# One planned order for every instruction of an attention and feed-forward kernel

## The chip, the cores and the metric

The kernel runs on one core of one Trainium2 chip. The metric is device microseconds (us) of that core, lower is better. The engines are PE (matrix products), DVE (vector), ACT (activation), POOL, and SP, which here only issues DMAs. Each engine works through its own queue strictly in order; semaphores tie the queues together.

## What is computed

```python
# batch 4, heads 12, sequence 448, head size 64; model 768, hidden 2048
scores = scale * q @ k^T                         # [4, 12, 448, 448]
scores = einsum('bhij,hg->bgij', scores, w_pre)  # mixes the heads
attn = softmax(scores, axis=-1)
attn = einsum('bhij,hg->bgij', attn, w_post)     # mixes the heads again
x = (attn @ v) as [1792, 768]
h = x @ w_in                                     # the feed-forward part
out = (h * sigmoid(1.702 * h)) @ w_out
```

The weights w_in and w_out arrive as 64-bit floats, the rest as 32-bit floats.

## The kernel before

**Attention in steps.** Mixing the heads is a matrix product over (query row, head) pairs, so a step takes 10 query rows of 12 heads, 120 partitions. A batch has 45 steps, the kernel 180. The scores of a batch are made in 4 chunks of 120 query rows (the last has 88): for each of 6 pairs of heads `scores` makes two products `qk` in PSUM (tag `gen`, 3 banks), `keep_scores` copies them to a tile `sc`, and `send_scores` writes that to a DRAM buffer `sd`. For a step, `gather` reads its 120 x 448 tile `r` back from `sd`, 4 steps ahead (`AHEAD`). Then: `mix` (PE, into one of 2 banks `mx`), `peak` (DVE, row maximum), `expo` (ACT, exponential and its sum), `shifted` (POOL) and `inverse` (DVE) for the reciprocal, `weigh_mix` (POOL) for the scaled second mixing matrix, `post_whole` (PE, `pp`), and `keep_whole` (ACT), which copies the result to the tile `p` of its chunk. Batches 0 and 1 do this in 32 bits. Batches 2 and 3 carry numbers as pairs of 16-bit floats, an upper and a lower part, each product being three 16-bit ones: `weigh`, `upper`, `lower`, `post`, `keep_upper`, `keep_lower`, and q, k, v are loaded, measured (`squares`) and split (`upper_part`, `lower_part`).

**Product with v.** When a chunk's steps are through, `context` multiplies `p` with v, one pair of heads (`pr`) per call, three calls sharing one PSUM bank `av`; `x_upper`, `x_lower` and `x_size` then take the bank to the 16-bit pair `x`. When all four chunks are there, `scale_x` sets a factor, and the batch's feed-forward part may begin.

**Feed-forward in quanta.** The hidden width is cut into 8 slices; a unit is one slice for one batch (32 units). A unit is 12 quanta on PE of six 128 x 448 products each: 2 x 3 for `hidden` (`h`) and 6 for `project` (`po`). Between them `gate` (ACT, DVE, ACT, DVE) makes `g`, and `collect` adds `po` to `acc`, on DVE alone or through ACT and POOL (`pt`). Each of the 16 weight slices is first converted once: `convert` loads 64-bit numbers (`w64`, three DMAs), makes 32-bit ones with five DVE instructions a part, splits them into a 16-bit pair and stores that to DRAM (`wd`); `fetch_w` reads the pair back for every unit (`wt`).

**What sets the order.** The program is written out in the order in which the instructions are to stand (`manual_schedule`). A loop over the steps lists each step's parts in a fixed order, with fixed lags (`LAG`). Side work (loads, conversions, splits) is a list of `jobs` with a first step, dependences in whole steps, and budgets of time (`tokens`) that each step refills. Feed-forward quanta are owed at `RATE` 2.15 per step. `slot` moves every chain (`gate`, `collect`, scores, context) one stage on. In the head, before step 0, the loads of q and k of batch 0 alternate with those of the first weight slice, and the second slice follows.

Of the kernel before, what the change touches and what calls it, by code (L numbers as in the profile page):

```python
# [39 lines left out]
def attention_then_feed_forward(ctx, tc, q, k, v, w_pre, w_post, w_in, w_out, out):  # L40
# [13 lines left out]
    AHEAD, LAG = 4, 3  # L54
    OVERLAP = True
# [58 lines left out]

    def sum_jobs(first, m, parts, after):

        t = {}

        def over():
            t["t"] = add_over(parts())  # L120

        j = job(first, None, 0, over, after=after, urgent=True)
        return job(first, "D", 0.2, lambda: add_along(m(), t["t"]), after=[j], urgent=True)
# [100 lines left out]
    open_banks = []  # L224

    def bank(name, tag="gen", bufs=3):

        if tag == "gen":
            while len(open_banks) >= bufs and not open_banks[-bufs]["done"]:
                slot()  # L230
            open_banks.append({"done": False})
        return ps.tile([128, 512], F32, name=name, tag=tag, bufs=bufs)

    def scores(b, c, pr, tag=("gen", 3)):
# [3 lines left out]
        done = open_banks[-2:] if tag[0] == "gen" else []  # L238
        w = NPAIR // THIRDS
        if b < WHOLE:  # L240
            qf, kf = st["q", b, pr // w], st["k", b, pr // w]
            for x in range(2):
                rs = slice(x * D, (x + 1) * D)
                nc.tensor.matmul(  # L244
                    two[x][:n, :S], qf[rs, pr % w, i0:i0 + n], kf[rs, pr % w, :],
                    start=True, stop=True,
                )
            return two, done
# [9 lines left out]
        return two, done  # L258

    def keep_scores(b, c, pr, two, engs, home=("sc", 3)):  # L260
        i0, n = chunk(b, c)
        t = flow.tile([CI, 2, S], F32, name=f"sc_{b}_{c}_{pr}", tag=home[0], bufs=home[1])
        for x in range(2):
            (nc.scalar.copy if engs[x] == "A" else nc.vector.tensor_copy)(t[:n, x, :], two[x][:n, :S])  # L264
        return t
# [84 lines left out]
    def upper(i):  # L350
        K = rows_of(steps[i][1])[1] * H
        a1 = flow.tile([KG, S], F16, name=f"a1_{i}", tag="a1", bufs=3)
        nc.scalar.activation(a1[:K], row.pop(("e", i))[:K], AF.Copy, scale=row.pop(("rs", i))[:K, 0:1])
        row["a1", i] = a1
# [116 lines left out]
    parts = []  # L471

    stores = []
    EARLY = -20

    def convert(kind, s, first):
# [80 lines left out]
        sizes = []  # L557
        for a in range(NP):
            n = len(parts) + a
            users = []  # L560
            begin = first + a if first == EARLY else first
            before = [(job(begin, None, 0, lambda a=a: fetch(a), stage=("w64", users)), 2)]
            before += [(parts[n - WF], 0)] if n >= WF else []
            for eng, cost, f in (
                ("D", 0.37, magnitude), ("D", 0.37, least), ("D", 0.37, shift), ("D", 0.8, rest), ("D", 0.8, sign),
            ):
                last = job(first, eng, cost, lambda f=f, a=a: f(a), after=before)
                users.append(last)
                before = [(last, 0)]
            sizes.append(job(first, "A", 0.7, lambda a=a: size(a), after=[(last, 1)]))  # L570
        j = sum_jobs(first, total, lambda: t["m"], [(x, 1) for x in sizes])
        j = job(first, "D", 0.9, scale_w, after=[(j, 0)])
        low = []
        for a in range(NP):
            up = job(first, "A", 0.72, lambda a=a: w_upper(a, "A"), after=[(j, 1)] + [(x, 0) for x in stores[-1:]])
            low.append(job(first, "D", 0.7, lambda a=a: w_lower(a), after=[(up, 1)]))
        parts.extend(low)
        stores.append(job(first, None, 0, store, after=[(x, 1) for x in low]))
        return stores[-1]
# [10 lines left out]
    def hidden(u, fc, part):  # L590

        s, b = units[u]
        if part == 0:
            st["h", u, fc] = bank(f"h_{u}_{fc}")[:, :S], open_banks[-1]
        h, _ = st["h", u, fc]
# [9 lines left out]
    def gate(u, fc):  # L605

        s, b = units[u]
        h, held = st.pop(("h", u, fc))
        if fc == 0:
            gt[u] = flow.tile([128, 2, SF, S], F16, name=f"g_{u}", tag="g", bufs=2)  # L610
            st["ct", u] = stat.tile([128, 2], F32, name=f"ct_{u}", tag="ct")
            nc.vector.tensor_scalar(
                st["ct", u][:, 0:1], ex[:, b:b + 1], ew[:, s, 0:1], 0.851 * 2.0 ** -13,
                op0=ALU.mult, op1=ALU.mult,
            )
        g = gt[u]
        th = flow.tile([128, S], F32, name=f"th_{u}_{fc}", tag="th", bufs=2)
        nc.scalar.activation(th, h, AF.Tanh, scale=st["ct", u][:, 0:1])  # L618
        spend("A", 0.55)
        yield  # L620
        nc.vector.scalar_tensor_tensor(th, th, 1.0, h, op0=ALU.add, op1=ALU.mult)  # L621
        held["done"] = True
        spend("D", 0.65)
        yield
        nc.scalar.activation(g[:, 0, fc], th, AF.Copy, scale=gs[:, b, 1:2])  # L625
        spend("A", 0.55)
        yield
        nc.vector.scalar_tensor_tensor(  # L628
            g[:, 1, fc], th, gs[:, b, 1:2], g[:, 0, fc], op0=ALU.mult, op1=ALU.subtract
        )  # L630
        spend("D", 0.65)

    def project(u, e):
        g, w = gt[u], wt[1, u].rearrange("p t (f e) -> p t f e", e=DM)
        po = bank(f"po_{u}_{e}")[:, :S]
        held = open_banks[-1]
# [6 lines left out]
        return po, held  # L643

    def collect(u, e, po, held):
        s, b = units[u]
        c = st["ct", u][:, 1:2]
        if e == 0:
            nc.vector.tensor_tensor(c, eo[:, b:b + 1], ew[:, s, 2:3], op=ALU.mult)
# [3 lines left out]
        held["done"] = True  # L653
        if s == 0:
            if tokens["A"] > tokens["D"]:
                nc.scalar.activation(a, po, AF.Copy, scale=c)
                spend("A", 0.55)
            else:
                nc.vector.tensor_scalar(a, po, c, 1.0, op0=ALU.mult, op1=ALU.mult)
                spend("D", 0.62)  # L660
        elif tokens["A"] > tokens["D"] + 0.3 and tokens["G"] > -1.0 and s < NS - 1:
            pt = flow.tile([128, S], F32, name=f"pt_{u}_{e}", tag="pt", bufs=2)
            nc.scalar.activation(pt, po, AF.Copy, scale=c)  # L663
            spend("A", 0.55)
            yield
            nc.gpsimd.tensor_tensor(a, a, pt, op=ALU.add)  # L666
            spend("G", 1.3)
        else:
            nc.vector.scalar_tensor_tensor(a, po, c, a, op0=ALU.mult, op1=ALU.add)  # L669
            spend("D", 0.65)  # L670
        if s == NS - 1:
            yield
            nc.sync.dma_start(out=out[e * 128:(e + 1) * 128, b * S:(b + 1) * S], in_=a)


    tokens = {"A": 0.0, "D": 0.0, "G": 0.0}

    def spend(eng, cost):
        tokens[eng] -= cost

    def refill(t):
        for e in tokens:
            tokens[e] = min(tokens[e] + t, 4.5)

    going = []

    def start(gen):

        going.append(gen)

    def slot():
        for g in list(going):
            if next(g, g) is g:
                going.remove(g)

    jobs = []

    stage_users = {"op": [], "w64": []}

    def stage_free(tag):  # L700

        u = stage_users[tag]
        return len(u) < THIRDS or all("at" in j for j in u[-THIRDS])

    def job(first, eng, cost, f, after=(), stage=None, urgent=False):
        j = {"urgent": urgent, "first": first, "eng": eng, "cost": cost, "f": f, "stage": stage,
             "after": [a if isinstance(a, tuple) else (a, 1) for a in after]}
        jobs.append(j)
        return j

    def run_jobs(i):
        more = True
        while more:
            more = False
            for j in list(jobs):
                if j["first"] > i or any(a.get("at", 10 ** 6) + lag > i for a, lag in j["after"]):
                    continue
                if j["stage"] is not None:
                    tag, users = j["stage"]
                    if not stage_free(tag):  # L720
                        continue
                    stage_users[tag].append(users)
                eng = j["eng"]
                if isinstance(eng, dict):
                    eng = max(eng, key=lambda e: tokens[e] - eng[e])
                    cost = j["eng"][eng]
                else:
                    cost = j["cost"]
                if eng and tokens[eng] < cost * 0.5 and not j["urgent"]:
                    continue  # L730
                if eng:
                    spend(eng, cost)
                j["f"](eng) if isinstance(j["eng"], dict) else j["f"]()
                j["at"] = i
                jobs.remove(j)
                more = True


    SENT = 2

    def staged(first, after, name, b, i, use):
# [348 lines left out]
```

## Time and profile before

| | |
|---|---|
| time, median of 3 runs | 991.54 us (990.67 to 992.24) |
| profiled execution | 991.19 us, of which the profiled span is 989.3 us |
| PE busy | 921.2 us of the span (93%) |
| DVE, ACT, POOL busy | 588.6, 581.7, 313.8 us |
| DMA | 196.74 MB, mean 199 GB/s |

The span is what the trace covers; the execution's own time is 1.9 us more. PE is the busiest engine by far. Its idle time, and what it waits for, are read by stage in the rows below, because DMA is dense early and thin late.

### The profile page before, as it was taken

The numbers are of one execution on the slowest core, as the hardware profiler recorded it, in microseconds if no ns is written. First come the engines' busy times: TensorE is split into PE (matmuls) and PEld (weight loads), VectorE is DVE, ScalarE is ACT, GpSimd is POOL, SyncE is SP. The second block draws the span as 40 slices with busy tenths as digits, with TensorE's granted clock in tenths as the row PEclk, the third lists the DMA queues.
The fourth block names the chain that finished last, engine by engine and source line by source line (L and its number), as shares of the span: only waits on it lengthen the run. The fifth ranks groups of instructions, "written<-read, shape, count | busy, mean of one in ns | idle before, by whom it ended". The sixth has DMA issues, their size and how long they took to land.

```text
span 989.3 us, 18926 instructions
## 1 busy us (share of the span) xinstructions
PE 921.2 (93%) x6972; PEld 544.9 (55%) x6972; DVE 588.6 (59%) x1333; ACT 581.7 (59%) x1342; POOL 313.8 (32%) x500
## 2 busy tenths in 40 slices
PE   6688899988999999997998999998999999999998
PEld 4345565654555556564564656564555666555554
DVE  5677776667658976456556575556555555442333
ACT  2577668775677667666567666556465555223331
POOL 0122222221113423445443543335435353001221
PEclk8799999999999999999999999999999999999999
DMA  8999878976778785557666575456645332153322
GB/s 302 284 324 320 292 265 266 316 249 189 242 251 272 252 262 181 182 170 214 198 199 222 164 223 156 143 161 199 212 133 167 103 118 65 65 183 129 104 88 88
DMA packets 66175, 196.74 MB, mean 199 GB/s; under 512 B 7620, under 2 KB 32324, under 8 KB 66084
## 3 DMA queue, kind: packets, MB, share of 16 engines
q1 hardware_dynamic: 65680, 195.46, 61.0%
q8 instruction: 55, 0.90, 0.4%
q10 hardware_dynamic: 404, 0.09, 0.1%
q14 instruction: 36, 0.29, 0.1%
HBM read 138.89 MB, written 56.62 MB: 198 GB/s over the span
## 4 chain that ended last, share of the span: by engine, by line
PE 67%; DVE 16%; ACT 8%; DMA 5%; issue 3%; POOL 0%; ACTq 0%; SPq 0%; DVEq 0%
PE h L600 19%; PE po L639 19%; PE mx L290 9%; PE pp L335 4%; PE av L424 3%; PE av L413 3%; PE qk L244 2%; PE qk L254 2%; DVE nm L297 2%; DVE w_f L510 2%; ACT e L304 2%; PE pp L372 2%; PE pp L374 2%; PE pp L373 2%; DVE w_f L516 2%
## 5 line engine op out<-in xcount | busy, mean ns | idle before, releaser
L639 PE MATMUL po<-g,wt 128*128 128x448 f16 x1152 | 243.4, 355 | 13.6 <-DVE th L621 8.6
L600 PE MATMUL h<-x,wt 128*128 128x448 f16 x1152 | 241.0, 354 | 4.9 <-ACT sc L264 3.7
L290 PE MATMUL mx<-r,wa 120*120 120x448 f32 x360 | 178.3, 578 | 26.0 <-ACT e L304 16.5
L304 ACT ACTIVATE e<-mx,nm 120x448 f32<-120x448 f32 x180 | 115.6, 642 | 139.8 <-DVE rs L320 130.5
L639 PEld LDWEIGHTS <-wt 128*128 128x128 f16 x1152 | 109.8, 99 | 126.9 <-issue 42.0
L600 PEld LDWEIGHTS <-wt 128*128 128x128 f16 x1152 | 109.3, 98 | 112.6 <-issue 24.2
L669 DVE SCALAR_TENSOR_TENSOR acc<-po,ct,acc 128x448 f32<-128x448 f32 x131 | 89.1, 681 | 71.4 <-PE po L639 69.9
L359 POOL TENSOR_TENSOR a<-w,a 120x448 f16<-120x448 f32 (+1 forms) x90 | 95.9, 1065 | 102.8 <-issue 46.7
L297 DVE TENSOR_REDUCE nm<-mx 120x1 f32<-120x448 f32 x180 | 110.6, 615 | 16.4 <-PE mx L290 16.3
L618 ACT ACTIVATE th<-h,ct 128x448 f32<-128x448 f32 x64 | 40.4, 632 | 133.8 <-PE h L600 117.9
L621 DVE SCALAR_TENSOR_TENSOR th<-th,h 128x448 f32<-128x448 f32 x64 | 39.6, 619 | 128.2 <-ACT th L618 128.2
L335 PEld LDWEIGHTS pp<-wr,e 120*112 120x112 f32 x720 | 89.0, 180 | 36.5 <-issue 30.4
L264 ACT COPY sc<-qk 120x448 f32<-120x448 f32 (+1 forms) x186 | 89.6, 532 | 31.9 <-PE qk L244 22.4
L325 POOL TENSOR_SCALAR wr<-wp,rs 120x120 f32<-120x120 f32 (+1 forms) x90 | 54.8, 609 | 166.7 <-DVE rs L320 119.8
L345 POOL TENSOR_SCALAR w<-e,rs 120x448 f32<-120x448 f32 (+1 forms) x90 | 66.0, 733 | 124.5 <-DVE rs L320 70.5
L290 PEld LDWEIGHTS mx<-r,wa 120*120 120x120 f32 x360 | 60.0, 187 | 67.2 <-ACT e L304 30.6
L315 POOL TENSOR_SCALAR rs<-sm 120x1 f32<-120x1 f32 x180 | 46.7, 260 | 142.0 <-ACT e L304 132.3
L335 PE MATMUL pp<-wr,e 120*112 120x120 f32 x720 | 90.3, 269 | 0.0
L666 POOL TENSOR_TENSOR acc<-acc,pt 128x448 f32<-128x448 f32 x37 | 43.6, 1179 | 129.6 <-ACT pt L663 128.7
L372 PE MATMUL pp<-wp,a 120*112 120x120 f16 x360 | 62.4, 217 | 3.8 <-DVE p L399 1.9
L320 DVE RECIPROCAL rs<-rs 120x1 f32<-120x1 f32 x180 | 28.1, 156 | 61.8 <-POOL rs L315 61.6
L628 DVE SCALAR_TENSOR_TENSOR g<-th,gs,g 128x448 f16<-128x448 f32 x64 | 50.3, 785 | 20.8 <-ACT g L625 19.8
(126 smaller groups left out, 1337.5 us busy)
## 6 DMA issues: line engine op xcount, KB each, us to landing
wt<-wd SPq DMA_DIRECT2D x64, 768.0 KB
r<-sd SPq DMA_DIRECT2D x176, 210.0 KB
sd<-sc SPq DMA_DIRECT2D x72, 420.0 KB
w<-in_moe_w_in_dram SPq DMA_DIRECT2D x24, 512.0 KB
w<-in_moe_w_out_dram SPq DMA_DIRECT2D x24, 512.0 KB
wd<-w_p SPq DMA_DIRECT2D x16, 768.0 KB
sd<-sc SPq DMA_DIRECT2D x24, 308.0 KB
out_dram<-acc SPq DMA_DIRECT2D x24, 224.0 KB
```

Of the source, the lines that this page charges most:

```text
L264: (nc.scalar.copy if engs[x] == "A" else nc.vector.tensor_copy)(t[:n, x, :], two[x][:n, :S])
L290: nc.tensor.matmul(mx[:K, :S], st["wa", b][:K, :K], row.pop(("r", i))[:K, :], start=True, stop=True)
L297: nc.vector.tensor_reduce(nm[:K], row["mx", i][:K, :S], axis=AX.X, op=ALU.max, negate=True)
L304: nc.scalar.activation(e[:K], row.pop(("mx", i))[:K, :S], AF.Exp, bias=row.pop(("nm", i))[:K, 0:1], scale=1.0, accum_out=sm[:K, 0:1],)
L325: nc.gpsimd.tensor_scalar(t[:K], wp[:K], row.pop(("rs", i))[:K, 0:1], 1.0, op0=ALU.mult, op1=ALU.mult)
L335: nc.tensor.matmul(pp[:CP, jc * K:(jc + 1) * K], e[:K, jc * CP:(jc + 1) * CP], wr[:K, :, :n], start=True, stop=True,)
L345: nc.gpsimd.tensor_scalar(w[:K], e[:K], row["rs", i][:K, 0:1], 1.0, op0=ALU.mult, op1=ALU.mult)
L359: nc.gpsimd.tensor_tensor(a2[:K], row.pop(("w", i))[:K], row["a1", i][:K], op=ALU.subtract)
L372: nc.tensor.matmul(o, a1[:K, js], wp1[:K, :, :n], start=True, stop=False)
L600: nc.tensor.matmul(h, w[:, i, c, fc * 128:(fc + 1) * 128], x[:, j, c, :], start=(n == 0), stop=(n == len(terms) - 1),)
L639: nc.tensor.matmul(po, w[:, j, fc, e * 128:(e + 1) * 128], g[:, i, fc, :], start=(n == 0), stop=(n == len(terms) - 1),)
L669: nc.vector.scalar_tensor_tensor(a, po, c, a, op0=ALU.mult, op1=ALU.add)
```

## The change

All scheduling code (`job`, `run_jobs`, `slot`, `tokens`, `do_quantum`) goes. Every piece of work becomes a task with its engine or a choice of engines, the time that it holds the engine (`occ`), the time until its result may be used (`lat`), the buffers that it takes, and a due step. `run_all` replays these on model clocks and writes out one task after another: on each engine, among the tasks that could start within 0.1 us of the earliest, the one with the earliest due step; of all engines the one that starts first. DMAs are modelled too, at 0.31 MB a us and with 8 in flight. The work itself is that of before, with these differences:

- Head: q and k of batch 0 are loaded first and alone; the conversions of weights begin in step 1 (slice n at 7n instead of 7n - 12, the first two before step 0). The scores of chunk 0 are sent in two parts, rows 0 to 47 of all six pairs, then the first four gathers, then the other rows. The three small loads of w_pre and w_post move from ACT's queue to SP's.
- The three calls of `context` for a bank are one task.
- Copies of scores may go to ACT or DVE, results to DVE or to ACT and POOL, splits to POOL or ACT, as the plan finds. Against before, ACT makes 150 score copies instead of 186 and DVE 42 instead of 6; 64 additions of `pt` run on POOL instead of 37, and 104 on DVE instead of 131.
- The feed-forward part is due from step 57 at 2.13 quanta a step.

```diff
-    OVERLAP = True
+    AHEAD = 4
...
-    def send_scores(b, c, pr, t):
-        n = chunk(b, c)[1]
-        nc.sync.dma_start(out=sd[b, c][:, 2 * pr:2 * pr + 2, :], in_=t[:n])
+    def send_scores(b, c, pr, t, lo=0, hi=CI):
+        hi = min(hi, chunk(b, c)[1])
+        nc.sync.dma_start(out=sd[b, c][lo:hi, 2 * pr:2 * pr + 2, :], in_=t[lo:hi])
...
+    def run_all():
+        last = ""
+        while waiting:
+            picks = []
+            for e in list(free) + ["-"]:
+                best = []
+                for j in waiting:
+                    if e not in j["eng"]:
                         continue
+                    room = room_for(j, e)
+                    if room is None:
+                        continue
+                    s = max(room, j["from"], free.get(e, 0.0))
+                    if j["size"] and len(lanes) >= 8:
+                        s = max(s, lanes[-8])
+                    best.append((s + (j["bias"] if e != j["eng"][0] else 0.0), s, j))
+                if best:
+                    t = min(x[0] for x in best) + LOOK
+                    picks.append(min((x for x in best if x[0] <= t), key=lambda x: (x[2]["due"], x[0]))[1:] + (e,))
+            s, j, e = min(picks, key=lambda x: (x[0], x[1]["due"]))
...
     for i in range(THIRDS):
         for name in "kq":
             load_whole(name, 0, i)
-        run_jobs(EARLY + i)
...
     for pr in range(NPAIR):
-        two, done = scores(0, 0, pr, tags[pr % 3])
-        send_scores(0, 0, pr, keep_scores(0, 0, pr, two, "AD", homes[pr]))
+        two = scores(0, 0, pr, tags[pr % 3])
+        kept.append(scores_home(0, 0, pr, homes[pr]))
+        for x in range(2):
+            keep_scores(0, 0, x, kept[pr], two, "AD"[x])
+        send_scores(0, 0, pr, kept[pr], 0, FRONT)
...
     for i in range(AHEAD):
         gather(i)
-    for i in range(THIRDS):
-        load_whole("v", 0, i)
+    for pr in range(NPAIR):
+        send_scores(0, 0, pr, kept[pr], FRONT)
...
+            def product(half=half, t=t):
+                for pr in range(3 * half, 3 * half + 3):
+                    t["av"] = context(b, c, pr)
```

**SP's queue in the head.** These are the last sends of chunk 0's scores (`sd`), the loads of the second weight slice (`w`), and the first gathers (`r`); the same stretch of before and of the change:

```order
L269 DMA sd_0_90<-sc_0_4_216 120x896
L269 DMA sd_0_90<-sc_0_5_224 120x896
L489 DMA w_0_64_0_234<-in_moe_w_out_dram 128x1024
L489 DMA w_0_64_1_237<-in_moe_w_out_dram 128x1024
L489 DMA w_0_64_2_239<-in_moe_w_out_dram 128x1024
L280 DMA r_241<-sd_0_90 120x448
L280 DMA r_243<-sd_0_90 120x448
```

```order
L250 DMA sd_0_90<-sc_0_4_190 48x896
L250 DMA sd_0_90<-sc_0_5_198 48x896
L261 DMA r_215<-sd_0_90 120x448
L261 DMA r_217<-sd_0_90 120x448
L261 DMA r_219<-sd_0_90 120x448
L261 DMA r_221<-sd_0_90 120x448
L250 DMA sd_0_90<-sc_0_0_158 72x896
```

Behind the shorter sends come the gathers at once; the other 72 rows of each send follow them, and the weights stand further back.

**PE's queue in batch 0, chunk 0 before and chunk 1 after.** `av` is the product with v, `mx` a step's mixing, `pp` its second mixing, `qk` scores:

```order
L413 MATMUL av_0_0_884<-p_0_417,vf_0_251 64x120 x8
L290 MATMUL mx_982<-r_848,wa_255 120x448
L335 MATMUL pp_984<-wr_949,e_907 112x120 x4
L413 MATMUL av_0_3_1009<-p_0_417,vf_0_251 64x120 x8
L290 MATMUL mx_1025<-r_894,wa_255 120x448
L335 MATMUL pp_1027<-wr_996,e_946 112x120 x4
L244 MATMUL qk_3_1_0_1053<-kf_0_122,qf_0_124 88x448
L244 MATMUL qk_3_1_1_1054<-kf_0_122,qf_0_124 88x448
L413 MATMUL av_0_3_1009<-p_0_417,vf_0_253 64x120 x8
```

```order
L271 MATMUL mx_1106<-r_1019,wa_203 120x448
L394 MATMUL av_1_0_1113<-p_1_799,vf_0_364 64x120 x16
L394 MATMUL av_1_0_1113<-p_1_799,vf_0_409 64x120 x8
L271 MATMUL mx_1160<-r_1027,wa_203 120x448
L316 MATMUL pp_1173<-wr_1156,e_1141 112x120 x4
```

Three runs of 8 products with other work between them have become one run of 24.

**DVE's queue where v of batch 2 is split.** `vp` is the lower part of v, `th` and `g` belong to `gate`, `nm` and `rs` to a step, `p` is `keep_lower`:

```order
L297 TENSOR_REDUCE nm_5231<-mx_5181 120x1
L320 RECIPROCAL rs_5196<-rs_5196 120x1
L212 SCALAR_TENSOR_TENSOR vp_2_5198<-vb_2_5110,s_v_4359,vp_2_5198 112x1024
L212 SCALAR_TENSOR_TENSOR vp_2_5200<-vb_2_5112,s_v_4359,vp_2_5200 112x1024
L212 SCALAR_TENSOR_TENSOR vp_2_5202<-vb_2_5114,s_v_4359,vp_2_5202 112x1024
L612 TENSOR_SCALAR ct_5289<-ex,ew 128x1
L621 SCALAR_TENSOR_TENSOR th_0_5291<-th_0_5291,h_0_5248 128x448
```

```order
L201 SCALAR_TENSOR_TENSOR vp_2_5194<-vb_2_5091,s_v_4204,vp_2_5194 112x1024
L576 SCALAR_TENSOR_TENSOR th_0_5230<-th_0_5230,h_0_5143 128x448
L301 RECIPROCAL rs_5245<-rs_5245 120x1
L201 SCALAR_TENSOR_TENSOR vp_2_5249<-vb_2_5096,s_v_4204,vp_2_5249 112x1024
L586 SCALAR_TENSOR_TENSOR g_5271<-th_0_5230,gs,g_5271 128x448
L278 TENSOR_REDUCE nm_5301<-mx_5251 120x1
```

The three long splits no longer stand together; `th`, for which the projections wait, has moved in between.

## Rows read from the trace of the kernel before

**Rows 1.** Page, part 1: busy us (share of the span) xinstructions.
```profile
span 989.3 us, 18926 instructions
...
PE 921.2 (93%) x6972; PEld 544.9 (55%) x6972; DVE 588.6 (59%) x1333; ACT 581.7 (59%) x1342; POOL 313.8 (32%) x500
```

**Rows 2.** Page, part 4: the chain that ended last, by engine.
```profile
PE 67%; DVE 16%; ACT 8%; DMA 5%; issue 3%; POOL 0%; ACTq 0%; SPq 0%; DVEq 0%
```

**Rows 3.** Five stretches: start:end, length, then what the first row names.
```profile
core 0: us, PE busy (x) PEld busy (x) DVE busy (x) ACT busy (x) POOL busy (x), PEclk, DMA share, GB/s
0.00:31.00 31.00, 16.40 (x79) 11.35 (x79) 18.10 (x47) 7.37 (x16) 0.70 (x7) 0.81 0.90 305
31.00:199.60 168.60, 148.57 (x980) 93.14 (x980) 121.63 (x309) 123.85 (x313) 38.97 (x103) 0.97 0.87 294
199.60:357.00 157.40, 146.33 (x944) 87.75 (x943) 114.16 (x273) 106.23 (x257) 38.82 (x68) 0.97 0.73 239
357.00:824.90 467.90, 450.27 (x3908) 267.62 (x3907) 270.40 (x578) 292.91 (x667) 205.89 (x294) 0.99 0.57 176
824.90:989.30 164.40, 159.66 (x1066) 85.07 (x1064) 64.31 (x129) 51.38 (x90) 29.40 (x29) 1.00 0.32 109
```

**Rows 4.** Waits of PE, 31 to 199.6, then to the end: total, times, longest.
```profile
PE mx L290 <- ACT e L304: 15.3, 17, 1.7
...
PE po L639 <- DVE th L621: 8.6, 5, 3.6
```

**Rows 5.** SP's issues and PE's first mixing in the head: start, us, what.
```profile
19.99 2.99 SPq L489 DMA_DIRECT2D w<-in_moe_w_out_dram  x3
24.48 2.20 SPq L280 DMA_DIRECT2D r<-sd  x4
...
30.90 3.31 PE L290 MATMUL mx<-r,wa 120*120 120x448 f32 x4 [7.97 <-DMA r<-sd]
```

**Rows 6.** Gathers issued up to 183 us; mixings (two records each) up to 206 us.
```profile
L280 SPq DMA_DIRECT2D r<-sd x52: 316/360/1263, 24.5 to 182.3; - x52
...
L290 PE MATMUL mx<-r,wa x108: 539/627/1071, 30.9 to 200.1; 120*120 120x448 f32 x106, 96*96 96x448 f32 x2
```

**Rows 7.** PE in order of time, three pieces: start us, us, what.
```profile
131.63 0.98 PE L335 MATMUL pp<-wr,e 120*112 120x120 f32 x8
132.54 1.04 PE L413 MATMUL av<-p,vf 112*64 112x120 f32 x16
133.51 1.01 PE L290 MATMUL mx<-r,wa 120*120 120x448 f32 x2
134.36 0.98 PE L335 MATMUL pp<-wr,e 120*112 120x120 f32 x8
...
222.07 0.98 PE L335 MATMUL pp<-wr,e 120*112 120x120 f32 x8
222.89 3.57 PE L600 MATMUL h<-x,wt 128*128 128x448 f16 x18
...
440.40 0.92 PE L290 MATMUL mx<-r,wa 120*120 120x448 f32 x2
441.16 1.30 PE L639 MATMUL po<-g,wt 128*128 128x448 f16 x6
```

**Rows 8.** DVE, then PE, about 460 us in order of time.
```profile
458.05 5.71 DVE L212 SCALAR_TENSOR_TENSOR vp<-vb,s_v,vp 112x1024 f16<-112x1024 f32 x3
...
465.33 3.65 PE L639 MATMUL po<-g,wt 128*128 128x448 f16 x12 [3.58 <-DVE th L621]
```

**Rows 9.** One line of DVE and one of POOL: ns min/median/max.
```profile
L628 DVE SCALAR_TENSOR_TENSOR g<-th,gs,g x64: 662/683/1556, 235.4 to 978.3; 128x448 f16<-128x448 f32 x64
...
L666 POOL TENSOR_TENSOR acc<-acc,pt x37: 1129/1132/1590, 285.2 to 979.5; 128x448 f32<-128x448 f32 x37
```

More of the change, by code (lines that the diff above doesn't have):

```diff
@@ L247, in scores @@
                 )
-            return two, done
+            return two
         qp, kp = st["qp", b, pr // w], st["kp", b, pr // w]
@@ L555, in store @@
             nc.sync.dma_start(out=wd[kind, s], in_=t["p"])
[L557 to L579, printed above, removed]
+        return {"fetch": fetch, "magnitude": magnitude, "least": least, "shift": shift, "rest": rest, "sign": sign,
+                "size": size, "total": total, "parts": lambda: t["m"], "scale_w": scale_w, "w_upper": w_upper,
+                "w_lower": w_lower, "store": store}
     units = [(s, b) for b in range(B) for s in range(NS)]
@@ L678, in spend @@
[L678 to L703, printed above, removed]
@@ new lines, in take, with settle @@
+    def take(j, e):
+        for x in j["takes"]:
+            if len(x) == 2 or x[2] == e:
+                have = held[x[0]]
+                if len(have) >= COUNT[x[0]]:
+                    done = [(over_when(h), n) for n, h in enumerate(have) if over_when(h) is not None]
+                    have.pop(min(done)[1])
+                have.append(x[1])
+    def settle(j, at, e, gap):
+        j["at"] = at
+        for x in j["next"]:
+            x["left"] -= 1
+            if not x["left"]:
+                waiting.append(x)
+        for x in j["then"]:
+            x["from"] = max(x["from"], at + (0.0 if e == "-" else SAME if x["eng"] == (e,) else gap))
+            x["left"] -= 1
+            if not x["left"]:
+                waiting.append(x)
@@ new lines, in score_tasks, with product, place @@
+    def score_tasks(b, c, pr, x):
+        third = pr // (NPAIR // THIRDS)
+        banks, sc, t = [[], []], [], {}
+        def product():
+            t["two"] = scores(b, c, pr)
+        def place():
+            t["t"] = scores_home(b, c, pr)
+        j = add("PE", 0.84 if b < WHOLE else 0.61, product,
+                gated_by(x) + [inputs.get((n, b, third)) for n in "kq"], x + 0.2, takes=[("gen", h) for h in banks], kind="qk")
+        for n in "kq":
+            in_home[n, b, third].append(j)
+        h = add("-", 0.0, place, [j], x + 0.3, 0.0, takes=[("sc", sc)])
+        both = []
+        for n in range(2):
+            k = add("A/D", {"A": 0.42, "D": 0.53}, lambda e, n=n: keep_scores(b, c, n, t["t"], t["two"], e), [h], x + 0.3,
+                    {"A": 0.53, "D": 0.62}, bias=0.3)
+            banks[n].append(k)
+            both.append(k)
+        s = add("SP", 0.4, lambda: send_scores(b, c, pr, t["t"]), both, x + 2, size=0.43)
+        sc += both + [s]
+        sends.setdefault((b, c), []).append(s)
```

702 lines of the change are left out of this document (382 added, 320 removed).

## The prediction, made before the changed kernel ran

> **What bounds the kernel now.** I read the busy shares first, then the chain, then the stretches, then the waits. PE is busy 93% of the span [rows 1] and holds 67% of the chain that ended last, against 16% for DVE and 5% for DMA [rows 2]: the end is set by how early PE gets through its work. But the mean hides stages. In the stretches [rows 3] the reader is to compare PE's busy time with the length, and then DMA's share: up to 199.6 us, when the 54th of 180 mixings starts [rows 6], DMA engines are 0.87 to 0.90 busy at about 300 GB/s and PE idles 34.6 us (14.6 of them in the first 31); from 357 us on PE idles 22.4 us in 632, and DMA is at 0.57 and below. So the first fifth is limited by DMA and PE together, the rest by PE. The waits [rows 4] say what PE lacks: early the exponential of a step (15.3 us in 17 waits; two banks for mixings, so a mixing waits for the exponential two steps back), later mostly `th`, the gate of the feed-forward part.
>
> **The change part by part.** The work is the same, so no instruction's price goes away; what can change is what stands ahead of what. Four terms.
>
> *1. The head and the first 53 mixings.* Before, the first gather is issued at 24.48 us, behind three loads of the second weight slice that take SP 2.99 us to issue, and the first mixing, which waited 7.97 us for the gathers, starts at 30.9 [rows 5]. By the queue's order six weight loads (6 x 0.524 = 3.15 MB by their shape) leave the front; at the 305 GB/s of that stretch [rows 3] they are 10.3 us. The first sends shrink to 48 of 120 rows, but the rest follows right behind the gathers and delays the fifth gather, and PE must still make the last scores first. I take 9 us for the head at the least. The other bound is DMA's: adding up the shapes of all DMAs ahead of the 53rd gather gives 55.6 MB before and 50.9 MB after, since conversions begin later. Before, 52 gathers were out by 182.3 us [rows 6], the 53rd by about 184 (estimate), 0.302 MB a us; at that rate 4.7 MB less are 15 us. Between 9 and 15 I take 12: PE would have to do its 148.6 us of work of the second stretch [rows 3] in about 163 us instead of 168.6, 91% instead of 88%, which needs only a third of the 15.3 us of waits for exponentials to go. If those waits stay, it is 9.
>
> *2. Products with v in threes, and fewer changes of kind.* The reader is to take start-to-start times [rows 7]. `pp` ahead of a product with v takes 0.91 us (131.63 to 132.54), ahead of `h` 0.82 (222.07 to 222.89); a mixing behind a product with v takes 0.85 (133.51 to 134.36), behind `po` 0.76 (440.40 to 441.16). So entering or leaving a run of `av` or `qk` costs about 0.09 us each way. PE's queue has 340 such borders before and 234 after; from the 54th mixing on, 246, and 159 after the change from the same place (its first `h`). 87 x 0.09 = 7.8 us; the other 19 are part of term 1. The cost is a later start of the bank's first copy, by two products of 0.97 us [rows 7]; one bank serves `av`, but a chunk lasts 12 steps, so this is hidden.
>
> *3. Work done ahead.* At that place 24 products with v (pairs of heads) are done instead of 20, and 50 second mixings instead of 49: 4 x 0.88 + 0.82 = 4.3 us less are left, 0.88 being the single run's 0.97 less one border. The feed-forward part starts there, behind 53 mixings, and not behind 60. From mixing 60 to 180 both orders place 253 quanta, so the pace per step stays; 5 more quanta are already done before, inside these steps' gaps.
>
> *4. Stalls behind 199.6 us.* PE idles 11.1 + 17.6 + 4.7 us in the last three stretches [rows 3]; the last 4.7, in which nearly only feed-forward work is left, I count as staying. Of the 28.7, the most telling piece is at 460 us [rows 8]: three splits of v hold DVE 5.71 us without a break, `th` waits behind them, and PE stands 3.58 us. The planned queue puts `th` and steps between those splits. PE pays twice: the 12 `po` behind this gap took 3.65 us, where 18 `h` take 3.50 elsewhere [rows 7]. The granted clock is 0.97 and 0.99 in the two stretches [rows 3], 4.7 us lost in each (0.03 x 157.4 and 0.01 x 467.9). A plan on fixed durations cannot remove all of this: I take half of the idle time (14.3) and half of the clock's (4.7), 19 us, with bounds of 0 and 38.
>
> What the plan moves between engines I cost at nothing: 36 score copies go from ACT to DVE and 27 additions from DVE to ACT and POOL, on engines that are 59%, 59% and 32% busy [rows 1]. If PE waits for them it costs up to their own length each, about 0.7 us. One row speaks against more work on POOL: the lower part of g on DVE has a median of 683 ns and a maximum of 1556, and POOL's addition takes 1132 [rows 9], so now and then DVE seems held for most of a POOL instruction. The Trainium skill, SBUF — State Buffer, section SBUF: two separate sides, says that a DVE operation with two SBUF inputs and a POOL operation that reads SBUF lock each other out for a whole instruction; by it 27 more additions could hold DVE 27 x 1.13 = 31 us, were each to meet one. By the row most do not (the median stands near the minimum). I keep it out of the sum, as DVE idles 400 us.
>
> Sum, on the profiled span: 989.3 - 12 - 7.8 - 4.3 - 19 = 946.2; the execution's time is 1.9 us more than its span (991.19 against 989.3), and the median of the runs, 991.54, agrees with it. **948 us**, 4.4% faster.
>
> **The rivals.**
>
> *The plan holds almost to the letter.* The estimate for the start becomes 20 us (the 15 by DMA, and some more from the exponentials' waits), and all of term 4's 38 goes: 989.3 - 20 - 7.8 - 4.3 - 38 + 1.9 = 921. For it: the plan's durations for PE are those of the rows (its code has 0.84 us for `pp`, the rows 0.82). Against: it has one number per instruction where DVE's spread is twofold [rows 9], and one rate for DMA.
>
> *Only the switches are saved.* Real latencies differ from planned ones, and in strict queues each error becomes a stall of the old size: terms 1 and 4 are zero. 989.3 - 7.8 - 4.3 + 1.9 = 979.
>
> *DMA falls behind the plan, and the kernel is slower.* The plan counts on 0.31 MB a us. Ahead of the 90th gather stand 96.2 MB after the change (102 before). Rows 3 give 9.5 + 49.6 + 37.6 = 96.7 MB moved by 357 us, 0.271 MB a us; the 90th gather of before went out at about 370 us (estimate: 102 MB, less than 8 DMAs in flight). If the new mixture of reads and writes moved only the 0.239 of the third stretch, the gather would come at 402 us, 32 later. About 14 us of terms 2 and 4 lie behind that place, so 989.3 + 32 - 14 + 1.9 = 1009. It decides from an average rate below 96.2 / 384 = 0.25 MB a us. For it: mixings, and all behind them on PE, wait for gathers in order. Against: the 0.239 was measured while PE was 93% busy and asked for no more, and 0.294 and 0.305 are seen where more was asked [rows 3].
>
> *No change.* Stalls moved, not removed, and the head's gain lost in the wait for later conversions: by the queues' order the last slice's weights are now fetched two steps ahead of their first use, where it was three. It gives 990.
>
> **How the numbers follow.** Forecast 0.50 (its own range 935 to 965), plan to the letter 0.20, only switches 0.17, DMA behind 0.10, no change 0.03. The predicted time is the forecast's. The range leaves out the slower rival (0.10) and the low edge of the best case (0.10): 918 to 985. About 0.2% is what a measurement of this kernel can tell from no change; faster by more than that 0.87, within it 0.03, slower 0.10.
>
> **What would show it.** Term 1: the first mixing at about 22 us, the first `h` at about 188, and DMA still near 0.9 busy until then. Term 2: PE's start-to-start times as above, `av` in runs of three at about 0.9 us a pair. Term 4: PE's idle time behind the first `h` at about 19 us instead of 33, the waits for `th` at a few us, a granted clock nearer 1.00. The prediction is wrong if gathers end PE's waits through the first 350 us, if PE's idle time stays or grows behind the first `h`, or if PE's work on the same products takes longer than now.

## The result, and the profile after

The changed kernel takes 930.92 us (median of 4 runs, 929.78 to 934.01), the kernel before 991.89 (990.67 to 994.66): a ratio of 0.9387 [0.9356, 0.9418]. The forecast of 948 us was 17 us too high, and its own range of 935 to 965 missed the time by 4; the whole range of 918 to 985 held it. The profiled execution took 930.12 us, 928.4 of them span, 60.9 less than before.

The page, part 1 and part 4, against [rows 1, 2]:

```profile
span 928.4 us, 18998 instructions
...
PE 897.2 (97%) x6972; PEld 535.5 (58%) x6972; DVE 589.4 (63%) x1342; ACT 593.3 (64%) x1328; POOL 337.8 (36%) x532
...
PE 75%; DVE 9%; DMA 6%; ACT 5%; issue 2%; POOL 2%; SPq 1%; ACTq 0%; POOLq 0%; DVEq 0%
```

PE makes the same 6972 products, but is busy 24.0 us less and idle 31.2 us instead of 68.1. DVE's share of the chain fell from 16% to 9%. Five stretches, columns as in [rows 3]; they end at the first mixing, at the first `h`, and then where like parts of the program end:

```profile
0.00:19.00 19.00, 13.89 (x76) 10.36 (x77) 6.27 (x19) 4.68 (x8) 0.71 (x7) 1.00 0.73 229
19.00:180.50 161.50, 147.95 (x1027) 93.13 (x1028) 117.26 (x300) 116.80 (x292) 35.69 (x101) 0.96 0.91 302
180.50:330.00 149.50, 146.78 (x959) 90.09 (x959) 129.19 (x318) 113.60 (x277) 43.38 (x78) 1.00 0.87 285
330.00:768.00 438.00, 433.94 (x3928) 259.61 (x3925) 284.16 (x601) 298.94 (x653) 213.57 (x305) 1.00 0.61 191
768.00:928.40 160.40, 154.60 (x996) 82.29 (x990) 52.49 (x108) 59.32 (x100) 44.46 (x42) 1.00 0.32 109
```

The first `h`, which here follows 53 mixings, starts at 180.5 us; before, the 54th mixing started at 199.6. That is 19.1 us; the rest of the gain lies behind this place. The same view of everything behind it, first of the kernel before, then of the changed one:

```profile
199.60:989.30 789.70, 756.25 (x5916) 440.44 (x5914) 448.87 (x979) 450.52 (x1013) 274.12 (x390) 0.99 0.55 174
```

```profile
180.50:928.40 747.90, 735.33 (x5871) 431.99 (x5869) 465.84 (x1025) 471.87 (x1029) 301.41 (x424) 1.00 0.60 192
```

41.8 us less, of which 21.0 are PE's busy time and 20.8 its idle time (33.4 to 12.6). In the second stretch DMA moves 302 GB/s, before 294: the rate is hardly higher. The granted clock is 1.00 behind the first `h`, but 0.96 in the second stretch, before 0.97.

The waits of PE, whole run (total, times, longest), against [rows 4]:

```profile
PE pp L316 <- POOL wr L306: 6.0, 10, 1.1
PE mx L271 <- DMA r<-sd: 3.1, 2, 2.7
PE h L557 <- DMA wt<-wd: 2.9, 1, 2.9
...
PE po L595 <- DVE th L576: 2.4, 3, 1.4
...
PE mx L271 <- ACT e L285: 1.9, 3, 0.8
```

The wait for exponentials fell from 15.3 us in the early stretch alone to 1.9, that for `th` from 8.6 to 2.4. None of those left is over 6 us in all. The head in order of time, against [rows 5]:

```profile
16.14 1.68 SPq L261 DMA_DIRECT2D r<-sd  x4
...
19.00 0.98 PE L271 MATMUL mx<-r,wa 120*120 120x448 f32 x2 [2.66 <-DMA r<-sd]
```

The gathers leave 8.3 us earlier, and the first mixing starts 11.9 us earlier. PE around a product with v, against [rows 7]:

```profile
109.50 0.98 PE L316 MATMUL pp<-wr,e 120*112 120x120 f32 x8
110.42 2.68 PE L394 MATMUL av<-p,vf 112*64 112x120 f32 x48
113.32 1.07 PE L316 MATMUL pp<-wr,e 120*112 120x120 f32 x8 [0.23 <-POOL wr L306]
114.23 0.92 PE L271 MATMUL mx<-r,wa 120*120 120x448 f32 x2
```

Three pairs of heads now stand in one run of 2.68 us, 0.89 a pair; before, a pair took 0.97 with its border.

### The profile page after: what moved, and what is told of

It is laid out like the page before. It is cut to its first block, busy times and chain, and to the rows that moved or that the text cites. A ratio compares the mean times of both kernels' runs of the same rounds, so it can differ in the third digit from the quotient of the medians.

```text
span 928.4 us, 18998 instructions
## 1 busy us (share of the span) xinstructions
PE 897.2 (97%) x6972; PEld 535.5 (58%) x6972; DVE 589.4 (63%) x1342; ACT 593.3 (64%) x1328; POOL 337.8 (36%) x532
## 4 chain that ended last, share of the span: by engine, by line
PE 75%; DVE 9%; DMA 6%; ACT 5%; issue 2%; POOL 2%; SPq 1%; ACTq 0%; POOLq 0%; DVEq 0%
PE po L595 20%; PE h L557 20%; PE mx L271 12%; PE pp L316 5%; PE av L394 3%; PE av L405 3%; PE qk L225 3%; PE qk L235 3%; DMA r<-sd 2%; PE pp L353 2%; PE pp L355 2%; PE pp L354 2%; DVE nm L278 2%; ACT e L285 1%; ACT waste L96 1%
## 5 line engine op out<-in xcount | busy, mean ns | idle before, releaser
L557 PE MATMUL h<-x,wt 128*128 128x448 f16 x1152 | 246.8, 352 | 3.2 <-DMA wt<-wd 2.9
L271 PE MATMUL mx<-r,wa 120*120 120x448 f32 x360 | 172.3, 563 | 5.2 <-DMA r<-sd 3.1
L623 POOL TENSOR_TENSOR acc<-acc,pt 128x448 f32<-128x448 f32 x64 | 72.8, 1138 | 117.3 <-ACT pt L617 116.9
L340 POOL TENSOR_TENSOR a<-w,a 120x448 f16<-120x448 f32 (+1 forms) x90 | 95.8, 1064 | 26.3 <-POOL w L326 17.6
L246 ACT COPY sc<-qk 120x448 f32<-120x448 f32 (+1 forms) x150 | 74.5, 532 | 15.7 <-PE qk L225 11.3
L619 DVE SCALAR_TENSOR_TENSOR acc<-po,ct,acc 128x448 f32<-128x448 f32 x104 | 70.3, 679 | 22.0 <-PE po L595 21.1
L326 POOL TENSOR_SCALAR w<-e,rs 120x448 f32<-120x448 f32 (+1 forms) x90 | 60.5, 672 | 40.8 <-DVE rs L301 35.0
L617 ACT ACTIVATE pt<-po,ct 128x448 f32<-128x448 f32 x64 | 40.6, 634 | 51.1 <-PE po L595 51.0
L334 ACT ACTIVATE a<-e,rs 120x448 f16<-120x448 f32 (+1 forms) x90 | 60.3, 670 | 18.4 <-DVE rs L301 17.2
L380 DVE TENSOR_TENSOR p<-pp,p 112x480 f16<-112x480 f32 (+1 forms) x90 | 58.4, 649 | 19.2 <-ACT p L376 18.9
L306 POOL TENSOR_SCALAR wr<-wp,rs 120x120 f32<-120x120 f32 (+1 forms) x90 | 47.4, 527 | 54.0 <-DVE rs L301 33.7
```

Source lines behind the costliest of these rows:

```text
L246: (nc.scalar.copy if eng == "A" else nc.vector.tensor_copy)(t[:n, x, :], two[x][:n, :S])
L271: nc.tensor.matmul(mx[:K, :S], st["wa", b][:K, :K], row.pop(("r", i))[:K, :], start=True, stop=True)
L326: nc.gpsimd.tensor_scalar(w[:K], e[:K], row["rs", i][:K, 0:1], 1.0, op0=ALU.mult, op1=ALU.mult)
L340: nc.gpsimd.tensor_tensor(a2[:K], row.pop(("w", i))[:K], row["a1", i][:K], op=ALU.subtract)
L557: nc.tensor.matmul(h, w[:, i, c, fc * 128:(fc + 1) * 128], x[:, j, c, :], start=(n == 0), stop=(n == len(terms) - 1),)
L623: nc.gpsimd.tensor_tensor(a, a, st.pop(("pt", u, e)), op=ALU.add)
```

## The experiments

Twelve kernels. A difference between two of them is that of their ratios to the kernel before, times 992 us; 0.003 in a ratio (3 us) is about half an interval's width.

**1. Products with v one at a time, the rest as changed** (337 borders on PE instead of 234; a border is a place in PE's queue where the kind of product changes to or from `av` or `qk`).

```diff
-                for pr in range(3 * half, 3 * half + 3):
-                    t["av"] = context(b, c, pr)
+            for pr in range(3 * half, 3 * half + 3):
+                def product(pr=pr, t=t):
+                    t["av"] = context(b, c, pr)
+                j = add("PE", 0.87 if whole else 0.6, product, ...)
```

> The changed kernel with its products with v planned one pair of heads at a time again (three tasks per bank, due 0.8 steps apart), all else replanned. PE's queue then has 337 borders of qk or av runs instead of 234. Theory of the borders (0.09 us each on a PE that is hardly idle): 103 x 0.09 = 9 us slower than 930.9, so 940, with PE's idle time about as it is (31 us in all). Rival 1, the products in threes gain nothing because PE's gaps swallow the borders: 931 +- 2. Rival 2, the longer hold of PE by a run of three was itself delaying the steps: 925 or less.

942.34 us, ratio 0.9476 [0.9443, 0.9509]: 8.8 us more than the changed kernel. PE in order of time (start, us):

```profile
102.42 1.04 PE L394 MATMUL av<-p,vf 112*64 112x120 f32 x16
103.39 1.01 PE L271 MATMUL mx<-r,wa 120*120 120x448 f32 x2
104.33 1.04 PE L394 MATMUL av<-p,vf 112*64 112x120 f32 x16
105.30 1.01 PE L271 MATMUL mx<-r,wa 120*120 120x448 f32 x2
106.15 0.98 PE L316 MATMUL pp<-wr,e 120*112 120x120 f32 x8
```

A mixing between two products with v takes 0.94 from start to start (103.39 to 104.33), one that only follows such a product 0.85 (105.30 to 106.15), as in [rows 7]. 103 more borders of 0.09 us make 9.3, and the median is 8.8 us longer: the price of a border agrees, and under the plan the end moves by about as much. The trace does not part it from the clock: PE is 14.4 us longer busy (911.6 against 897.2) at a granted clock of 0.985 instead of 0.992, and idles 2.5 us less.

**2. Products with v in threes, the rest as before.**

```diff
-at_context.setdefault(last + LAG + 2 + pr, []).append((b, c, pr))
+at_context.setdefault(last + LAG + 4 + 3 * (pr // 3), []).append((b, c, pr))
```

> The kernel before, order by hand, with three products with v of a bank put together in one step (the third step of before's three for the first bank, so that no due time moves earlier). 236 borders instead of 340. Theory of the borders: 104 x 0.09 = 9 us of PE time less, 981 to 985, if the run of three does not delay the steps. Rival, that the hand order's gaps swallow it, or that the bank's later copies give it back: 989 to 994.

988.81 us, 0.9973 [0.9957, 0.999]: 2.7 us gained by 104 fewer borders, where 9.4 were to come. That is at the edge of the rival's 989. PE's busy time fell by 5.7 us only (921.2 to 915.5), at a granted clock of 0.973 instead of 0.981, and these waits grew:

```profile
PE mx L290 <- ACT e L304: 20.4, 24, 3.1
PE po L639 <- DVE th L621: 9.8, 7, 3.6
```

PE's idle time as a whole grew by 1.5 us. That a run of 2.7 us pushes back the mixing behind it in the fixed order, and so makes these waits, is my reading. So term 2 exists by itself, but kept a third of its size without the plan; of what is missing, the trace has 3.7 us as busy time, at the lower clock, and 1.5 as idle time.

**3. The plan on wrong durations**, each multiplied by a random factor from 0.6 to 1.4.

```diff
+        wrong = rng.uniform(0.6, 1.4)
+        occ, lat = {e: o * wrong for e, o in occ.items()}, {e: o * wrong for e, o in lat.items()}
         j = {"eng": tuple(occ), "occ": occ, "lat": lat, "f": f,
```

> The changed kernel planned with wrong durations: each task's engine time and latency times a random factor between 0.6 and 1.4 (DMAs stay as they were). The work, the due steps and the buffers are the same, and 235 borders instead of 234. Theory that the plan's accuracy is what removed PE's idle time: the idle time goes back to the old size or above (68 us of the span before, 31 after the change), 965 to 985. Rival, that the graph with its due steps and small borders is enough and engine queues forgive errors of this size: within 1% of 930.9, below 940.

937.57 us, 0.9427 [0.9398, 0.9456]: 4.0 us more, and the intervals still overlap. The wait for `wr` grew to 10.9 us, the largest. My theory that accurate durations removed the idle time fell; an order from the graph of tasks and the due steps does most of it: in this trace PE idles 41.1 us, before 68.1 and with the right durations 31.2. It is one draw of the factors.

**4. The three lower splits of a tensor a step apart, the rest as before.**

```diff
-                         after=[(up, 1)], urgent=True)
+                         after=[(up, 1)] + ([(lo, 1)] if lo else []), urgent=True)
```

> The kernel before, order by hand, with the three lower parts of a split (k, q, v of batches 2 and 3) put at least one step apart on DVE instead of back to back. Theory of term 4's example: PE's gaps of 3.58 us at 465 and 3.47 us at 690 us, where th waits behind 5.7 us of splits, go, and with them the slow clock behind each (about 1.2 us each): 7 to 10 us less, 982 to 985. Rival, that the stall moves to whatever comes late next: 988 to 993.

983.34 us, 0.9909 [0.9889, 0.9928]: 9.0 us gained by this alone, as expected. At the place of [rows 8] in the kernel before, `th` needs `ct`, a small factor that DVE makes behind the three splits and ACT waits for (DVE, ACT, DVE):

```profile
463.69 0.20 DVE L612 TENSOR_SCALAR ct<-ex,ew 128x1 f32<-128x1 f32 x1
463.99 0.63 ACT L618 ACTIVATE th<-h,ct 128x448 f32<-128x448 f32 x1 [2.96 <-DVE ct L612]
464.65 0.62 DVE L621 SCALAR_TENSOR_TENSOR th<-th,h 128x448 f32<-128x448 f32 x1 [0.76 <-ACT th L618]
```

The wait for `th`, and DVE at this place, with the splits apart:

```profile
PE po L639 <- DVE th L621: 3.7, 5, 1.5
```

```profile
459.73 2.17 DVE L212 SCALAR_TENSOR_TENSOR vp<-vb,s_v,vp 112x1024 f16<-112x1024 f32 x1
461.82 0.20 DVE L612 TENSOR_SCALAR ct<-ex,ew 128x1 f32<-128x1 f32 x1
464.23 0.62 DVE L621 SCALAR_TENSOR_TENSOR th<-th,h 128x448 f32<-128x448 f32 x1 [2.21 <-ACT th L618]
469.19 1.27 DVE L212 SCALAR_TENSOR_TENSOR vp<-vb,s_v,vp 112x1024 f16<-112x1024 f32 x1
472.48 1.26 DVE L212 SCALAR_TENSOR_TENSOR vp<-vb,s_v,vp 112x1024 f16<-112x1024 f32 x1
```

`ct` and `th` now stand between the splits, `ct` behind one of them instead of three. The wait fell from 8.6 to 3.7 us. The traced execution was the slowest of six (986.34 us) and has 5.1 us of the gain: 3.5 between the 105th and the 110th mixing, where the place at 460 us lies, and 4.2 between the 140th and the 160th, where the like one at 690 lies; elsewhere it loses 2.6, at a granted clock of 0.977 instead of 0.981.

**5. The new head alone on the order of before** (q and k first, scores in two parts around the first gathers, the loads of v in the steps). Its conversions begin at the old steps, those of the first two slices at step 1. (54.9 MB stand ahead of the 53rd gather, before 55.6.)

```diff
-        run_jobs(EARLY + i)
...
-        send_scores(0, 0, pr, keep_scores(0, 0, pr, two, "AD", homes[pr]))
+        kept.append(keep_scores(0, 0, pr, two, "AD", homes[pr]))
+        send_scores(0, 0, pr, kept[pr], 0, FRONT)
...
+    for i in range(AHEAD):
+        gather(i)
+    for pr in range(NPAIR):
+        send_scores(0, 0, pr, kept[pr], FRONT)
...
-            begin = EARLY + 10 * n if n < 2 else 7 * n - 12 if n <= NS else 11 * (n - NS) // 2 + 7 * NS - 12
+            begin = max(7 * n - 12, 1) if n <= NS else 11 * (n - NS) // 2 + 7 * NS - 12
```

> The kernel before, order by hand, with the head of the change, but with the conversions of weights at their old steps (slice n at 7n - 12, the first three from step 1 or 2). It parts the two things that y1_head did together (1013 us): head and later conversions. Bytes ahead of the 5th gather 6.3 MB (before 10.7), of the 53rd 54.9 (55.6). Theory now that the head gives about 11 us at the first mixing, of which the hand order keeps 3 to 6 at the 54th, and that the later conversions caused the loss (PE waited 9.7 us for weights, and its clock fell to 0.96): 984 to 989. Rival, that the head itself is harmful under the hand order, as it lets score copies and first conversions meet: above 1000. Second rival, the prediction's term 1 in full: 975 to 980.

998.97 us, 1.0077 [1.0052, 1.0102]: 7.6 us slower than before. Both expectations of a gain fell; the rival of a harmful head, above 1000, came nearest. From the first to the 54th mixing, and behind it:

```profile
18.67:200.18 181.51, 153.72 (x980) 96.24 (x981) 128.09 (x323) 125.88 (x319) 41.58 (x104) 0.93 0.89 294
200.18:995.50 795.32, 758.92 (x5918) 441.25 (x5916) 455.15 (x992) 452.66 (x1017) 281.56 (x391) 0.98 0.56 175
```

The first mixing starts 12.2 us earlier than before, the 54th no earlier. Between them PE is 5.2 us longer busy with the same 980 products, at a granted clock of 0.93 instead of 0.97 [rows 3], and idles 7.8 us more; behind them it is 2.7 us longer busy and idles 2.9 more. Why the late part is slower stays open.

**6. The new head with the new, later conversions (slice n at 7n), on the order of before** (50.9 MB ahead of the 53rd gather).

```diff
+            begin = max(7 * n, 1) if n <= NS else 5 * (n - NS) + 7 * NS
```

> The kernel before, order by hand, with only the head and the start of the conversions taken from the change (q and k first, scores sent in two parts around the first gathers, v loads and conversions in the steps, slice n at 7n). Its DMA bytes ahead of the 5th and 53rd gather equal the change's (6.3 and 50.9 MB against 10.7 and 55.6). Theory of the prediction's term 1, that DMA and the head set the start: first mixing at about 19 us instead of 30.9, the 54th mixing 12 to 19 us earlier, and since PE is the bound behind it the same at the end: 972 to 980. Rival, that the steps' order on PE, DVE and ACT (15.3 us of waits for exponentials) limits these steps: the head's 11 us shrink to under 5 at the 54th mixing, 986 to 992.

1013.41 us, 1.0218 [1.0198, 1.0238]: 21.6 us slower, both expectations missed. PE's waits, and the stretch in the middle:

```profile
PE h L600 <- DMA wt<-wd: 9.7, 2, 7.6
...
PE pp L372 <- DVE p L399: 7.1, 7, 3.8
```

```profile
357.00:846.00 489.00, 451.82 (x3936) 268.73 (x3933) 287.91 (x614) 300.11 (x683) 214.33 (x298) 0.96 0.56 173
```

PE stands 37.2 us in this stretch, before 17.6 [rows 3]: weights come too late for `h`, as the last rival said. Its granted clock is 0.96, before 0.99, and in the whole trace PE is 8.8 us longer busy with the same products. Yet the early stretch gained. The last start of the 54 first row maxima (`nm`, one a step) tells the pace; in turn the kernel before, experiment 5, experiment 6 and the changed kernel:

```profile
L297 DVE TENSOR_REDUCE nm<-mx x54: 602/617/626, 35.8 to 205.4; 120x1 f32<-120x448 f32 x53, 96x1 f32<-96x448 f32 x1
```

```profile
L297 DVE TENSOR_REDUCE nm<-mx x54: 605/617/626, 20.4 to 204.1; 120x1 f32<-120x448 f32 x53, 96x1 f32<-96x448 f32 x1
```

```profile
L297 DVE TENSOR_REDUCE nm<-mx x54: 601/617/625, 19.6 to 197.6; 120x1 f32<-120x448 f32 x53, 96x1 f32<-96x448 f32 x1
```

```profile
L278 DVE TENSOR_REDUCE nm<-mx x54: 604/624/626, 20.0 to 185.3; 120x1 f32<-120x448 f32 x53, 96x1 f32<-96x448 f32 x1
```

Of the 20.1 us between first and last, the head brings 1.3 (the 15 us of its earlier start are lost again), the 4.0 MB of later conversions 6.5, and the planned order with its products in threes the remaining 12.3. By the start of the 54th mixing itself (199.6, 200.2, 193.1 and 183.5 us) the three are -0.6, 7.1 and 9.6.

**7. The plan with conversions as early as before** (7n - 12, not before 4n + 1; 55.2 MB ahead of the 53rd gather).

```diff
-        x = 7 * n if n <= NS else 7 * NS + 5 * (n - NS)
+        x = 7 * n - 12 if n <= NS else 11 * (n - NS) // 2 + 7 * NS - 12
+        x = max(x, 4 * n + 1)
```

> The changed kernel with the conversions of weights begun earlier, nearer to the old steps (slice n at 7n - 12 but not before 4n + 1). Ahead of the 53rd gather then stand 55.2 MB instead of 50.9, ahead of the 90th 101.2 instead of 96.2. Theory that DMA sets the pace of the first 180 us (0.91 busy at 302 GB/s there): 4.3 MB more are 14 us, the first h comes at about 194 us instead of 180.5, and the end moves by 10 to 14 us, to 941 to 945. Rival, that the order on PE and the steps' chain set the pace there: first h within 4 us of 180.5, the end at 928 to 934.

933.29 us, 0.9394 [0.937, 0.9418]: 0.7 us more, not to be told from no change. The theory that DMA's bytes set the time fell, though at the 54th maximum they cost 9.4 us:

```profile
L278 DVE TENSOR_REDUCE nm<-mx x54: 599/618/626, 21.0 to 194.7; 120x1 f32<-120x448 f32 x53, 96x1 f32<-96x448 f32 x1
```

The plan puts the first `h` behind 49 mixings here instead of 53, at 181.5 us, so PE does later work while gathers are late.

**8. The plan with conversions later still, evenly** (slice n at 14 + 36n/7).

```diff
-        x = 7 * n if n <= NS else 7 * NS + 5 * (n - NS)
+        x = 14 + 36 * n // 7
```

> The changed kernel with the conversions spread evenly, slice n at 14 + 36n/7 (before 7n, then every 5), so that the first slices come later and the last at the same step 91. Bytes ahead of the 53rd gather 49.7 MB instead of 50.9, ahead of the 90th 97.0 instead of 96.2; the first h stands behind 49 mixings instead of 53. An attempt at a version that beats both. Theory that DMA sets the pace up to the 90th gather, whatever the order: about the same, 927 to 934. Rival, that the early start of the feed-forward part is worth its 4 steps: 918 to 925.

933.56 us, 0.9416 [0.9395, 0.9437]: 2.9 us more, within the intervals. The first `h` starts at 173.1 us instead of 180.5, and the end does not move: an earlier first `h` is no gain by itself.

**9. The plan with the old head**: loads of the first weight slice among those of q and k, all 120 rows sent ahead of the gathers (`early` is that slice's conversion).

```diff
     for i in range(THIRDS):
         for name in "kq":
             load_whole(name, 0, i)
+        early["fetch"](i)
...
-    FRONT = 48
+    FRONT = CI
```

> The changed kernel, its order planned, with the old head: the three loads of the first weight slice alternate with those of q and k, and all 120 rows of the scores are sent ahead of the first gathers. Bytes ahead of the 5th gather 7.9 MB instead of 6.3, of the 53rd 50.9 as before. Theory that under the plan a later start moves everything behind it: first mixing at about 26 us instead of 19, the end 5 to 8 us later, 936 to 939. Rival, that the pace of DMA up to the 53rd gather makes it up (same bytes by then): 929 to 933.

936.47 us, 0.9443 [0.9417, 0.947]: 5.6 us more. The first `nm` comes at 28.5 us instead of 20.0, the 54th at 190.7 instead of 185.3; these 5.4 us stay to the end.

**10 to 12. No choice of engine: results on DVE and copies of scores on ACT (10), results alone (11), copies alone (12).**

```diff
-            eng = "D" if s == NS - 1 else "D/A"
+            eng = "D"
...
-            k = add("A/D", {"A": 0.42, "D": 0.53}, lambda e, n=n: keep_scores(...)
+            k = add("A", {"A": 0.42}, lambda e="A", n=n: keep_scores(...)
```

> The changed kernel without a choice of engine for copies of scores (all ACT) and for results of the projection (all DVE, no addition on POOL); splits keep their choice. Theory of the prediction, which priced the choice at nothing because these engines are below 65% busy: 930 to 935. Rival, that the choice is what keeps short-lived banks free (3 banks for qk, h and po): PE waits for score copies and results, 945 to 960.

> The changed kernel with all results of the projection on DVE (no addition on POOL), copies of scores still free to choose. With both choices fixed the kernel took 926.4 (0.9324 of before) against 930.9 (0.9387). Theory that the path over ACT and POOL is the worse half, since a result there takes ACT and then 1.13 us of POOL and can hold DVE up: 925 to 928, all of the gain. Rival, that the copies are it: 930 to 932.

> The changed kernel with all copies of scores on ACT, results of the projection still free to choose. The counterpart of z2_results. Theory that the results are the worse half: 930 to 932. Rival, that the copies are it, since DVE is the fuller engine in the first 330 us (its share there 0.73 to 0.86 of the time): 925 to 928.

926.44 us, 0.9324 [0.9302, 0.9346]; 925.02 us, 0.9327 [0.9302, 0.9353]; 932.45 us, 0.9401 [0.9376, 0.9426]. The choice for results costs 6 us, that for copies nothing that shows. Experiments 10 and 11 are the fastest of all, and their ratios do not tell them apart. The page of 11, part 1:

```profile
PE 895.4 (97%) x6972; PEld 534.2 (58%) x6972; DVE 631.9 (68%) x1417; ACT 546.1 (59%) x1251; POOL 264.4 (29%) x470
```

POOL and ACT are spared 73.4 and 47.2 us of work and DVE takes on 42.5, at the same count of products. Against the changed kernel's profile PE is 1.8 us less busy and 2.1 us less idle. But all queues are the same in these two kernels for the first 210 us, and there 11 is already 3.2 us ahead: executions of the same instructions differ by that much, so this pair of traces cannot place the 6 us. Experiments 10 and 12 can, as they differ in the results alone. At the 54th and the 70th mixing their traces agree within 0.01 us, 0.8 us lie between them at the 98th, 6.4 at the 100th and 7.4 at the last. Between the 98th and the 100th, `h` waits for weights in experiment 12, in 10 only for additions (whole run):

```profile
PE h L557 <- DMA wt<-wd: 4.9, 1, 4.9
```

```profile
PE h L557 <- DVE acc L619: 2.0, 2, 1.1
```

The changed kernel has this wait for weights too, 2.9 us; 10 and 11 do not. So in that pair most of the difference arises around one late slice of weights; why the results on ACT and POOL would delay it stays open.

## Why the prediction was right, and where its sizes were off

The mechanism was right in the main: PE's queue bounds the kernel, and a better order brings it closer to its busy time. The sizes were not: the four terms together gave 43.1 us of span, measured 60.9, and in term 1 the reasons were wrong as well.

**Term 1, 12 us, measured 19.1.** The step that was off is the choice between 9 and 15. The head was not worth 9 at the least: 1.3 us on the old order, and at the end a loss (experiment 5), 5.4 with the plan (experiment 9). The bytes were not worth 15: 4.0 to 4.3 MB moved the 54th maximum by 6.5 and 9.4 us (experiments 6, 7). What I had not priced is the order of the early steps, 10 to 12 us as the remainder in experiment 6; no run has it alone. Of the 15.3 us of waits for exponentials nearly all went. The working also mixed two bounds: 163 us for the second stretch belong to a start 15 us earlier, 12 us leave 165.7, and 4.7 MB at 0.302 MB a us are 15.6 us.

**Terms 2 and 3, 7.8 and 4.3.** Experiment 1 agrees with the price of a border. Term 3 counted at another place than term 1. It took the kernel before right behind the 53rd mixing, with 20 products with v and 49 second mixings done; at 199.6 us, from where term 1 is measured, one more of each is through:

```profile
197.08 1.01 PE L290 MATMUL mx<-r,wa 120*120 120x448 f32 x2
197.93 0.98 PE L335 MATMUL pp<-wr,e 120*112 120x120 f32 x8
198.84 0.83 PE L413 MATMUL av<-p,vf 112*64 112x88 f32 x16
199.60 1.01 PE L290 MATMUL mx<-r,wa 120*120 120x448 f32 x2
```

So only three pairs of the shorter last chunk are ahead, at 0.76 us (198.84 to 199.60): 2.3 us instead of 4.3. Behind the first `h` PE is busy 21.0 us less; terms 2 and 3 are then 10.1 of it, and the 10.9 left are near the 9.4 that [rows 3] lost to the clock. Term 3 was not tried by itself.

**Term 4, 19 us, measured about 30**: 20.8 of idle time and about 10 of these. I took half of each for fear that fixed durations miss; the plan took 62% of the idle time and, by the granted clock of 1.00 in all three stretches, nearly all of the clock's loss. Experiment 3 shows why the fear was too large: durations wrong by up to 40% cost 4 us. Experiment 4 shows that the gap of [rows 8] was the right one to look at, though what stood behind the splits was first `ct`. That PE lacked "mostly `th`" later was too much: 8.6 of 33.4 us, the largest wait but a quarter.

**The choice of engines, nothing**: wrong by about 6 us (experiments 10, 11). It is a loss that the larger gains hid.

**The rivals.** "Only the switches" fell with term 4. "DMA behind" fell: gathers held PE 3.1 us in all, and even 4.3 MB more ahead of the 53rd were made good. "No change" by late weights did not occur here (2.9 us, once); experiment 6 has it in the wait of 9.7 us, and takes 14 us more than experiment 5, whose weights come earlier. "Plan to the letter", 921, came nearer in size than the forecast (10 us off against 17), with a chance of 0.20: term 1 was as it said, and 12.6 us of idle time behind the first `h`, where it left 4.7, kept it from the rest.

## What to carry to other kernels

With strict queues, price an order by what waits in it, not by bytes or by an earlier start: a head whose first mixing starts 12 us earlier was worth nothing on an order that could not use it. Look for long side instructions that stand together ahead of a short one on which the bound engine's work depends, even through another engine; setting three of them a step apart gained 9 us with one line. Here the plan needed the graph and the due steps more than exact durations, and a choice of engines that it is given should be timed without it.

## What the runs showed of the hardware

The same split of v, 112x1024, took 2.17 us on DVE in one place of experiment 4 and 1.27 and 1.26 in two others (above). POOL at these places, in order of time:

```profile
459.70 1.12 POOL L208 TENSOR_SCALAR vp<-vb,s_v 112x1024 f16<-112x1024 f32 x1
460.80 1.60 POOL L345 TENSOR_SCALAR w<-e,rs 120x448 f32<-120x448 f32 x1
...
469.37 1.59 POOL L345 TENSOR_SCALAR w<-e,rs 120x448 f32<-120x448 f32 x1 [4.25 <-DVE rs L320]
```

The slow split began 0.03 us behind POOL's of 1.12 us and took 0.90 longer; the fast one began 0.18 us ahead of a `w`, which then took 1.59 us, where `w` has a median of 0.64 in this run. Whichever begins first seems to hold the other. That is what the Trainium skill, SBUF — State Buffer, section SBUF: two separate sides, says of DVE with two SBUF inputs and POOL, and this trace agrees for these two pairs. The 5.71 us of the three splits in [rows 8] are 3 x 1.27 and 1.9 more. In the changed kernel the six splits of v have a median of 1.48 us, before 2.05. For `g` the other fear that I took from that page did not come true: with 64 additions on POOL instead of 37, it has a median of 684 ns and a maximum of 1354 on DVE, before 683 and 1556 [rows 9].
